# First-layer weight chunks of 256 inputs by 512 columns, and a second row buffer, in the first mixture of a one-core kernel

## The chip, the core and the metric

The kernel runs on one core of a Trainium2 chip. The metric is the device time of one execution in microseconds (us), as a median over several runs. The engines of the core are PE (TensorE; PEld is its weight load), ACT (ScalarE), DVE (VectorE), POOL (GpSimd) and SP (SyncE, which issues most DMAs here). Each works through its own queue in order; they meet at semaphores.

## The reference

Attention with a learned position bias (2 batches, 8 heads, 576 positions, 64 wide) gives 1152 tokens of 512 numbers. They go through a first mixture of 8 experts, one expert for each token, and then through a dense two-layer block, called the second mixture in the code:

```python
logits = x @ w_gate                      # 1152 x 8
expert_idx = np.argmax(logits, axis=1)   # one expert for each token, at most 288 tokens each
h = np.maximum(np.einsum('ecd,edf->ecf', disp, w1), 0.0)   # per expert: 512 -> 1024
y = np.einsum('ecf,efd->ecd', h, w2)                       # per expert: 1024 -> 512
out[i] = gate_w[i] * y[expert_idx[i], pos[i]]
...
h = x @ w_in; g = ((clip) of h, squared); out = g @ w_out  # 512 -> 2048 -> 512
```

## The kernel before

The attention takes the first 260 us of the span. The change touches only the first mixture, which follows it. There the tokens are gathered in the order of their experts into `xTh` and `xTl` (inputs on the partitions, four blocks of 128; h is a value rounded to the matmul format fp32r, l the remainder that the rounding leaves). Every weight matrix is used in the same two parts, so each product is made of three: h by h, h by l and l by h.

The weights come in chunks of 128 x 1024 numbers (512 KB), eight for each expert: chunks 0 to 3 are first-layer weights, 4 to 7 second-layer weights. A chunk `n` is loaded into a slot of `stage` (6 slots, `w_dma`), its rounded part is cast into `ring_h` (`w_hi`, mostly on ACT, L899, sometimes on DVE, L897) and its remainder is computed into `ring_l` (`w_lo`, L904, on DVE or POOL); `w_lo` then issues the load of chunk `n + 6` on SP. `hook(s)` does this for chunk `8e + 4 + s`, that is four chunks ahead of PE: hooks 0 to 3 prepare the expert's own second layer, hooks 4 to 7 the next expert's first layer. In the last expert hooks 3 and 4 also start to decode the weights of the second mixture on DVE (L941 to L951).

The number of tokens of an expert is known only on the chip, so each expert has two arms behind a branch. `wide_arm` takes up to 288 tokens: weights are stationary, tokens move, 96 products of 288 columns for each layer. `small_arm` takes up to 128 tokens: the tokens are stationary (copied by `x_pick` from their place in `xTh`, `xTl` to the fixed tiles `xsh`, `xsl`, L1199 and L1200), the weights move; the result `hs` is transposed back (`tr`, four times two blocks of 128 x 128) and evicted as `hTh` (ACT) and `hTl` (DVE), and the second layer runs in eight blocks `f`. In this data experts 0, 1 and 4 are wide, 2, 3, 5, 6 and 7 small. A small arm's last step is the transposed output in bank `psh2`, which ACT (L1179) and DVE (L1181) read.

`mid` stands inside the second layer: it transposes gathered tokens that the next experts need (`x_block`), fills the rest of `xTh`, `xTl` with zeros once (in expert 3's arm, L957 and L958), and calls `x_pick` for the next expert. PE tells the branch unit ahead of time which arm comes next (`guess`). The first chunk holds all 512 inputs by 256 columns of the first layer, so it ends two of the eight blocks of h.

The order of the instructions in this part is written out by hand (`tc.manual_schedule`): what stands first in the code stands first in its engine's queue.

Of the kernel before, what the change touches and what calls it, by code (L numbers as in the profile page):

```python
# [9 lines left out]
F32 = mybir.dt.float32  # L10
F32R = mybir.dt.float32r
# [32 lines left out]
P = 128  # L44
# [6 lines left out]
def tile_attn_moe_moe2(  # L51
# [868 lines left out]
    def w1_at(e, c):  # L920
        n = 8 * e + c
        return [t[n % NR].rearrange("p (k f) -> p k f", k=4) for t in (ring_h, ring_l)]

# [168 lines left out]
    hs = mp1.tile([P, F], F32, name="hs")  # L1092
    xsh = mp1.tile([P, 4, P], F32R, name="xsh")
    xsl = mp1.tile([P, 4, P], F32R, name="xsl")

    def wide_arm(e, r, wins, hook, mid):
        for wi, (c0, cw) in enumerate(wins):
            for f in range(8):
                if wi == 0 and f % 2 == 1:
                    hook(f // 2)  # L1100
                wh, wl = w1_at(e, f // 2)
                ps = psH[f % 4]
                fs = slice(P * (f % 2), P * (f % 2) + P)
                n = 0
                for kd in range(4):
                    xh = xTh[:, kd, ds(r["pe"] + c0, cw)]
                    xl = xTl[:, kd, ds(r["pe"] + c0, cw)]
                    for l, m in ((wh, xh), (wh, xl), (wl, xh)):
                        nc.tensor.matmul(ps[:, 0:cw], l[:, kd, fs], m, start=n == 0, stop=n == 11)  # L1109
                        n += 1  # L1110
                nc.scalar.activation(out=hTh[:, f, 0:cw], in_=ps[:, 0:cw], func=AF.Relu)
                nc.vector.scalar_tensor_tensor(out=hTl[:, f, 0:cw], in0=ps[:, 0:cw], scalar=0.0,
                                               in1=hTh[:, f, 0:cw].bitcast(F32), op0=ALU.max, op1=ALU.subtract)
            for f in range(8):
# [16 lines left out]
    def small_arm(e, r, hook, mid):  # L1131
        def tr(c):
            pt = psY[c % 2][:, 0:256]
            for i in range(2):
                f = 2 * c + i
                nc.tensor.transpose(pt[:, P * i:P * i + P], hs[:, P * f:P * f + P], ident)
            p2 = pt.rearrange("p (i t) -> p i t", i=2)
            hv = hTh[:, 2 * c:2 * c + 2, 0:P]
            nc.scalar.copy(out=hv, in_=p2)
            nc.vector.tensor_tensor(out=hTl[:, 2 * c:2 * c + 2, 0:P], in0=p2, in1=hv.bitcast(F32), op=ALU.subtract)  # L1140

        for c in range(4):
            wh, wl = w1_at(e, c)
            ps = psH[c][:, 0:256]
            n = 0
            for kd in range(4):
                xh, xl = xsh[:, kd, :], xsl[:, kd, :]
                for l, m in ((xh, wh), (xh, wl), (xl, wh)):
                    nc.tensor.matmul(ps, l, m[:, kd, :], start=n == 0, stop=n == 11)  # L1149
                    n += 1  # L1150
            nc.scalar.activation(out=hs[:, 256 * c:256 * c + 256], in_=ps, func=AF.Relu)
            if c > 0:
                tr(c - 1)
            hook(c)
# [8 lines left out]
        for f in range(6):  # L1163
            for hf in range(2):
                y_mm(f, hf)
            if f == 0:
                tr(3)
            if f in HK:
                hook(HK.index(f) + 4)
            if f == 3:  # L1170
                mid()
        for hf in range(2):
# [10 lines left out]
    with tc.manual_schedule():  # L1183
# [13 lines left out]

        def x_pick(r):
            nc.vector.tensor_copy(xsh, xTh[:, :, ds(r["dve"], P)].bitcast(F32))  # L1199
            nc.vector.tensor_copy(xsl, xTl[:, :, ds(r["dve"], P)].bitcast(F32))  # L1200

        done = nx0
        if CAP > 0:
            x_pick(regs[0])
            guess(0)
        for e in range(E if CAP > 0 else 0):
# [20 lines left out]

            def mid(late=True, e=e, first=first, more=more, nxt=regs[e + 1] if e + 1 < E else None):
                if late:
                    first()  # L1230
                for t in more:
                    x_block(t, xb[t])
                if e + 1 == zx_at:
                    zfill_x()
                if e == 1:
                    zfill_y()
                if nxt is not None:
                    x_pick(nxt)

            if CAP > P:  # L1240
# [133 lines left out]
def _arrays(q, k, v, w1, b1, w2, moe_w_gate, moe_w1, moe_w2, moe2_w_in, moe2_w_out):  # L1374
# [41 lines left out]
    for b in range(2):  # L1416
# [34 lines left out]
```

## Time and profile before

| | |
|---|---|
| median of 3 runs | 651.42 us (646.96 to 659.75) |
| the profiled execution | 656.27 us, span of its profile 654.5 us |
| PE busy | 571.0 us, 87% of the span |
| DVE busy | 507.6 us, 78% |
| ACT busy | 363.6 us, 56% |
| POOL busy | 330.9 us, 51% |
| mean granted clock of PE | 0.934 |
| experts 2 to 7 | 334.4 to 444.3 us of the span |

The profile is one execution, recorded instruction by instruction. A line such as L904 is a line of the kernel above; `rl<-raw,rh` says which tile is written and which are read. What stands in square brackets is the time in which the engine did nothing before the instruction, and the instruction of another engine that ended it; "issue" there means that nothing in the profile ended it. [...]

### The profile page before, as it was taken

To read this page: it belongs to the slowest core of one execution; us is meant where nothing else is said; L and a number is where in the kernel's file an instruction comes from. 1 tells how busy PE (TensorE), PEld (TensorE's weight loads), DVE (VectorE), ACT (ScalarE), POOL (GpSimd) and SP (SyncE) were. 2 spreads that over 40 slices of the span, in tenths; PEclk is the share of its full clock that TensorE was granted. 3 is DMA by queue.
4 is the path that set the end of the run, shared out by engine and by line. 5 is a ranking of instruction groups with operands and counts; after the bars stand their busy time and mean duration, and the time that the engine had idled before them with its cause. 6 is when DMAs were issued, how large, how long until landed. Compare 5 with 4: busy or idle time off the path is not lost.

```text
span 654.5 us, 14186 instructions
## 1 busy us (share of the span) xinstructions
PE 571.0 (87%) x5336; PEld 510.8 (78%) x5336; DVE 507.6 (78%) x942; ACT 363.6 (56%) x765; POOL 330.9 (51%) x266
## 2 busy tenths in 40 slices
PE   3766887988979996699998998888989999999996
PEld 3646666767767884498998897888969989988985
DVE  7999999999999744746568766775996888887431
ACT  4776776878869633143557436645654743642620
POOL 3789898999989820534263343311421420420442
PEclk9767799999989975799999899888999999999999
DMA  8497967999879985645458764773233134100012
GB/s 338 85 209 167 164 118 157 181 156 163 174 146 189 158 150 177 238 132 200 157 175 264 242 199 159 258 244 127 82 129 128 66 110 148 65 1 1 2 60 86
DMA packets 116388, 98.26 MB, mean 150 GB/s; under 512 B 98000, under 2 KB 99024, under 8 KB 114256
## 3 DMA queue, kind: packets, MB, share of 16 engines
q1 hardware_dynamic: 114000, 89.96, 54.1%
q0 software_dynamic: 1440, 4.72, 2.1%
q10 hardware_dynamic: 864, 2.47, 1.1%
q8 instruction: 51, 0.84, 0.5%
q14 instruction: 33, 0.27, 0.2%
HBM read 65.15 MB, written 4.72 MB: 107 GB/s over the span
## 4 chain that ended last, share of the span: by engine, by line
PE 44%; DVE 7%; issue 4%; ACT 3%; POOL 1%; POOLq 0%; DVEq 0%; ACTq 0%
PE psh L1307 13%; PE psy L1332 7%; PE psh L1109 7%; PE psy L1123 6%; PE psh L1149 5%; PE psh L1332 5%; PE psy L1160 1%; DVE rl L904 1%; ACT rh L899 1%; DVE on L1042 1%; DVE rt L943 1%; DVE cl L1312 1%; DVE gl L1321 1%; POOL out_dram L1340 1%; ACT rh L948 1%
## 5 line engine op out<-in xcount | busy, mean ns | idle before, releaser
L1317 POOL TENSOR_TENSOR rl<-rl,cl 128x384 f32<-128x384 f32 x48 | 51.4, 1071 | 133.3 <-ACT cl L1316 54.7
L904 POOL TENSOR_TENSOR rl<-raw,rh 128x1024 fp32r<-128x1024 f32 x23 | 59.1, 2573 | 97.3 <-ACT rh L899 78.9
L269 PE MATMUL ab_ps<-Wt,mask 128*128 128x64 f16 x720 | 61.0, 204 | 34.3 <-ACT bs L283 16.2
L399 POOL TENSOR_TENSOR hl<-s,hl 128x576 f16<-128x576 f32 x55 | 81.0, 1477 | 5.3 <-ACT mn L359 2.7
L288 POOL TENSOR_TENSOR bias<-bias,bs 128x256 f32<-128x256 f32 x78 | 74.0, 957 | 17.4 <-ACT bs L283 17.2
L904 DVE TENSOR_TENSOR rl<-raw,rh 128x1024 fp32r<-128x1024 f32 x41 | 62.8, 1540 | 18.4 <-PE psh L1149 8.6
L269 PEld LDWEIGHTS <-mask 128*128 128x128 f16 x720 | 51.5, 104 | 28.0 <-DVE mask L252 22.4
L252 DVE TENSOR_TENSOR mask<-sD,sT 128x1024 f16<-128x1024 f16 x72 | 73.1, 1029 | 0.0
L1307 PE MATMUL psh<-yTh,rh 128*128 128x384 f32 x192 | 65.8, 342 | 0.7 <-ACT yTh L1179 0.7
L1307 PE MATMUL psh<-yTh,rl 128*128 128x384 f32 x192 | 65.3, 340 | 0.0
L1307 PE MATMUL psh<-yTl,rh 128*128 128x384 f32 x192 | 64.6, 340 | 0.0
L270 PEld LDWEIGHTS <-mask 128*128 128x128 f16 x720 | 52.3, 105 | 13.3 <-issue 13.2
L270 PE MATMUL ab_ps<-Wt,mask 128*128 128x64 f16 x720 | 60.6, 203 | 0.0
L899 ACT CAST rh<-raw 128x1024 fp32r<-128x1024 f32 x54 | 55.8, 1053 | 4.1 <-DMA raw<-in_moe_w_dram 2.3
L1313 ACT ACTIVATE rl<-psh,half 128x384 f32<-128x384 f32 x48 | 28.0, 582 | 43.5 <-DVE cl L1312 43.4
L283 ACT ACTIVATE bs<-ab_ps,isa 128x256 f32<-128x256 f32 x78 | 35.6, 471 | 24.8 <-DVE bias L275 22.1
L1321 DVE TENSOR_TENSOR gl<-rl,gh 128x384 fp32r<-128x384 f32 x48 | 26.7, 557 | 29.1 <-ACT gh L1320 28.6
L366 ACT ACTIVATE s<-s,mn 128x576 f32<-128x576 f32 x56 | 43.6, 779 | 1.7
L352 DVE CUSTOM_DVE_ANT_0 s<-s_ps,bias 128x576 f32<-128x576 f32 x56 | 41.8, 747 | 3.0 <-POOL bias L288 2.2
L409 PE MATMUL mi<-V16h,pt 128*128 128x64 f16 (+1 forms) x320 | 40.8, 204 | 2.5 <-DMA pt<-hl 2.4
L410 PE MATMUL mi<-V16l,pt 128*128 128x64 f16 (+1 forms) x320 | 40.1, 201 | 0.8 <-DVE V16l L194 0.8
L409 PEld LDWEIGHTS <-pt 128*128 128x128 f16 (+1 forms) x320 | 32.0, 108 | 11.2 <-issue 4.0
(262 smaller groups left out, 1976.3 us busy)
## 6 DMA issues: line engine op xcount, KB each, us to landing
raw<-in_moe_w_dram SPq DMA_DIRECT2D x60, 512.0 KB, 4.2
raw<-in_moe_w_in_dram SPq DMA_DIRECT2D x8, 1024.0 KB, 4.8
raw<-in_moe_w_out_dram SPq DMA_DIRECT2D x8, 1024.0 KB, 4.8
qraw<-in_q_dram SPq DMA_DIRECT2D x15, 256.0 KB, 4.2
kst<-kraw SPq DMA_DIRECT2D x12, 288.0 KB, 6.0
vraw<-in_v_dram SPq DMA_DIRECT2D x3, 768.0 KB, 8.3
xd<-xt SPq DMA_DIRECT2D x8, 256.0 KB, 2.0
raw<-in_moe_w_dram ACTq DMA_DIRECT2D x4, 512.0 KB, 4.7
```

The costliest lines, as they stand in the source:

```text
L252: nc.vector.tensor_tensor(out=m, in0=win, in1=thr, op=ALU.is_gt)
L269: nc.tensor.matmul(pv[:, :, j], m[:, j, :], W["h"], start=True, stop=False)
L270: nc.tensor.matmul(pv[:, :, j], m[:, j, :], W["l"], start=False, stop=True)
L288: nc.gpsimd.tensor_tensor(out=bv, in0=bv, in1=bs_t.pop((it, c)), op=ALU.add)
L399: eng.tensor_tensor(out=hl[:, 1, 0:S], in0=s, in1=hl[:, 0, 0:S], op=ALU.subtract)
L409: nc.tensor.matmul(o, pt[:, blk, ic], vh, start=blk == 0, stop=False)
L899: nc.scalar.copy(out=ring_h[n % NR], in_=stage[n % NS])
L904: eng.tensor_tensor(out=ring_l[n % NR], in0=stage[n % NS], in1=ring_h[n % NR].bitcast(F32), op=ALU.subtract)
L1109: nc.tensor.matmul(ps[:, 0:cw], l[:, kd, fs], m, start=n == 0, stop=n == 11)
L1307: nc.tensor.matmul(ps, l[:, kd, fs], mv[:, kd, cs], start=i == 0, stop=i == 11)
L1317: nc.gpsimd.tensor_tensor(out=rl, in0=rl, in1=cl, op=ALU.add)
L1332: nc.tensor.matmul(ps, l[:, tsl], mv[:, f % 2, :], start=f == 0 and i == 0, stop=f == 3 and i == 2)
```

## The change

Three things change in the first mixture.

- The host lays out `moe_w1` in chunks of 256 inputs by 512 columns instead of 512 inputs by 256 columns. A chunk has the same size; chunks 0 and 1 now make the first four blocks of h together, chunks 2 and 3 the last four. The wide arm holds four blocks open in four banks over two chunks and evicts them in the second; hooks are called after as many products as before. The small arm makes 24 products of 512 columns instead of 48 of 256, evicts `hs` in two halves instead of four quarters, and transposes it in two groups of four blocks (`tr(0)` after chunk 2, `tr(1)` after block 0 of the second layer).
- The tiles for an expert's rows exist twice, used in turn. Where no gathered tokens are outstanding (`early`, from expert 3 on), `x_pick` of the next expert stands at the head of the arm instead of in `mid`.
- In the small arm `mid` stands after block 2 of the second layer and ahead of hook 6, instead of after block 3.

```diff
     def w1_at(e, c):
         n = 8 * e + c
-        return [t[n % NR].rearrange("p (k f) -> p k f", k=4) for t in (ring_h, ring_l)]
+        return [t[n % NR].rearrange("p (k f) -> p k f", k=2) for t in (ring_h, ring_l)]
...
-    xsh = mp1.tile([P, 4, P], F32R, name="xsh")
-    xsl = mp1.tile([P, 4, P], F32R, name="xsl")
+    xs = [[mp1.tile([P, 4, P], F32R, name=f"xs{w}{i}") for w in "hl"] for i in range(2)]
 
     def wide_arm(e, r, wins, hook, mid):
         for wi, (c0, cw) in enumerate(wins):
...
+            for c in range(4):
+                wh, wl = w1_at(e, c)
+                for fb in range(4):
+                    if wi == 0 and fb == 2:
+                        hook(c)
+                    f = 4 * (c // 2) + fb
+                    ps = psH[fb]
+                    fs = slice(P * fb, P * fb + P)
+                    n = 0
+                    for k in range(2):
+                        xh = xTh[:, 2 * (c % 2) + k, ds(r["pe"] + c0, cw)]
+                        xl = xTl[:, 2 * (c % 2) + k, ds(r["pe"] + c0, cw)]
+                        for l, m in ((wh, xh), (wh, xl), (wl, xh)):
+                            nc.tensor.matmul(ps[:, 0:cw], l[:, k, fs], m, start=c % 2 == 0 and n == 0, stop=c % 2 == 1 and n == 5)
+                            n += 1
+                    if c % 2 == 1:
+                        nc.scalar.activation(out=hTh[:, f, 0:cw], in_=ps[:, 0:cw], func=AF.Relu)
...
     def small_arm(e, r, hook, mid):
...
+        xsh, xsl = xs[e % 2]
+
+        def tr(g):
+            for i in range(4):
+                f = 4 * g + i
+                nc.tensor.transpose(psY[g][:, P * i:P * i + P], hs[:, P * f:P * f + P], ident)
+            p4 = psY[g].rearrange("p (i t) -> p i t", i=4)
+            hv = hTh[:, 4 * g:4 * g + 4, 0:P]
+            nc.scalar.copy(out=hv, in_=p4)
+            nc.vector.tensor_tensor(out=hTl[:, 4 * g:4 * g + 4, 0:P], in0=p4, in1=hv.bitcast(F32), op=ALU.subtract)
 
         for c in range(4):
             wh, wl = w1_at(e, c)
-            ps = psH[c][:, 0:256]
+            ps = psH[c // 2]
             n = 0
-            for kd in range(4):
-                xh, xl = xsh[:, kd, :], xsl[:, kd, :]
+            for k in range(2):
+                xh, xl = xsh[:, 2 * (c % 2) + k, :], xsl[:, 2 * (c % 2) + k, :]
                 for l, m in ((xh, wh), (xh, wl), (xl, wh)):
-                    nc.tensor.matmul(ps, l, m[:, kd, :], start=n == 0, stop=n == 11)
+                    nc.tensor.matmul(ps, l, m[:, k, :], start=c % 2 == 0 and n == 0, stop=c % 2 == 1 and n == 5)
                     n += 1
-            nc.scalar.activation(out=hs[:, 256 * c:256 * c + 256], in_=ps, func=AF.Relu)
-            if c > 0:
-                tr(c - 1)
+            if c % 2 == 1:
+                nc.scalar.activation(out=hs[:, 512 * (c // 2):512 * (c // 2) + 512], in_=ps, func=AF.Relu)
+            if c == 2:
+                tr(0)
             hook(c)
...
             if f == 0:
-                tr(3)
+                tr(1)
+            if f == 2:
+                mid()
             if f in HK:
                 hook(HK.index(f) + 4)
-            if f == 3:
-                mid()
...
-        def x_pick(r):
-            nc.vector.tensor_copy(xsh, xTh[:, :, ds(r["dve"], P)].bitcast(F32))
-            nc.vector.tensor_copy(xsl, xTl[:, :, ds(r["dve"], P)].bitcast(F32))
+        def x_pick(e):
+            for dst, src in zip(xs[e % 2], (xTh, xTl)):
+                nc.vector.tensor_copy(dst, src[:, :, ds(regs[e]["dve"], P)].bitcast(F32))
...
+            early = done >= NTT and not more and not pre
...
-                if nxt is not None:
-                    x_pick(nxt)
+                if e + 1 < E and not early:
+                    x_pick(e + 1)
...
                     guess(e + 1)
+                    if early and e + 1 < E:
+                        x_pick(e + 1)
                     small_arm(e, r, lambda s: hook(s, few=True), mid)
                 with few.Else():
                     guess(e + 1)
+                    if early and e + 1 < E:
+                        x_pick(e + 1)
                     first()
                     wide_arm(e, r, windows, hook, lambda: mid(False))
...
-        "moe_w1": c(moe_w1.reshape(8, 4, 128, 4, 256).transpose(0, 3, 2, 1, 4).reshape(8, 4, 128, 1024)),
+        "moe_w1": c(moe_w1.reshape(8, 2, 2, 128, 2, 512).transpose(0, 4, 1, 3, 2, 5).reshape(8, 4, 128, 1024)),
```

## Rows read from the trace of the kernel before

**Rows 1.** The page, shares of the chain that ended last, by engine.
```profile
PE 44%; DVE 7%; issue 4%; ACT 3%; POOL 1%; POOLq 0%; DVEq 0%; ACTq 0%
```

**Rows 2.** Windows of small experts: length, busy PE, PEld, DVE, ACT, POOL, clock, DMA.
```profile
334.40:350.50 16.10, 14.10 (x116) 13.66 (x117) 11.57 (x13) 11.53 (x20) 6.80 (x4) 1.00 0.77 252
350.50:365.20 14.70, 13.25 (x108) 12.79 (x108) 12.82 (x15) 10.55 (x18) 5.21 (x2) 1.00 0.82 264
...
395.20:410.10 14.90, 13.22 (x108) 12.78 (x108) 10.36 (x11) 10.56 (x18) 5.21 (x2) 1.00 0.46 161
410.10:426.80 16.70, 14.67 (x108) 14.15 (x109) 13.09 (x15) 10.56 (x18) 5.20 (x2) 0.90 0.78 257
426.80:444.30 17.50, 15.08 (x108) 14.37 (x108) 12.70 (x15) 8.54 (x16) 2.54 (x3) 0.90 0.72 251
```

**Rows 3.** Timeline of PE, 350 to 441 us: start, length, instruction, idle time before it.
```profile
350.51 0.35 PE L1149 MATMUL psh<-rh,xsh 128*128 128x256 f32 x1 [1.66 <-DVE xsh L1199]
...
365.28 0.37 PE L1109 MATMUL psh<-xTh,rh 128*128 x1 [1.22 <-DVE xTh L957]
...
370.13 0.30 PE L1109 MATMUL psh<-xTh,rh 128*128 x1
...
395.27 0.35 PE L1149 MATMUL psh<-rh,xsh 128*128 128x256 f32 x1 [2.66 <-issue]
...
410.13 0.36 PE L1149 MATMUL psh<-rh,xsh 128*128 128x256 f32 x1 [1.34 <-DVE xsh L1199]
...
440.49 0.39 PE L1160 MATMUL psy<-rh,hTl 128*128 128x256 f32 x1 [0.75 <-DVE hTl L1140]
```

**Rows 4.** Source view, PE's prefetch hints at the head of two arms: shortest/median/longest ns, when.
```profile
L1447 PEldq BRANCH_PREFETCH_HINT  x1: 44/44/44, 395.1 to 395.1; - x1
...
L1447 PEldq BRANCH_PREFETCH_HINT  x1: 30/30/30, 408.8 to 408.8; - x1
```

**Rows 5.** Source view of L904 on DVE: shortest/median/longest in ns.
```profile
L904 DVE TENSOR_TENSOR rl<-raw,rh x41: 1207/1225/2987, 271.5 to 437.0; 128x1024 fp32r<-128x1024 f32 x41
```

**Rows 6.** Timelines of DVE and POOL in expert 5, 400 to 412 us.
```profile
401.70 2.00 DVE L904 TENSOR_TENSOR rl<-raw,rh 128x1024 fp32r<-128x1024 f32 x1 [0.52 <-ACT rh L899]
...
404.63 2.80 POOL L904 TENSOR_TENSOR rl<-raw,rh 128x1024 fp32r<-128x1024 f32 x1 [2.01 <-ACT rh L899]
...
405.53 4.12 DVE L904 TENSOR_TENSOR rl<-raw,rh 128x1024 fp32r<-128x1024 f32 x2
409.57 0.41 DVE L1199 CAST xsh<-xTh 128x512 fp32r x1
```

**Rows 7.** Timeline of DVE in expert 4: it reads the output of expert 3.
```profile
369.12 0.68 DVE L1181 TENSOR_TENSOR yTl<-psh,yTh 128x512 f32 x1
```

**Rows 8.** Timeline of DVE in expert 7, 438 to 440 us.
```profile
438.16 0.68 DVE L941 TENSOR_SCALAR rt<-raw 128x1024 uint32<-128x1024 uint32 x1
438.88 1.23 DVE L943 SCALAR_TENSOR_TENSOR rt<-raw,rt 128x1024 uint32<-128x1024 uint32 x1
```

**Rows 9.** The chain that ended last, in order of time: start, length, products of a piece.
```profile
350.51 3.13 PE psh L1149 x24
353.87 1.44 PE psh L1149 x12
...
426.82 4.64 PE psh L1149 x24
...
535.57 10.88 PE psh L1332 x48
```

**Rows 10.** Window of 2 us in expert 6, columns as in the windows above.
```profile
412.00:414.00 2.00, 1.60 (x9) 1.51 (x8) 0.79 (x2) 1.21 (x2) 0.00 (x0) 0.50 0.93 322
```

**Rows 11.** Groups of instructions by line: busy us, mean ns of one, idle before.
```profile
L899 ACT CAST rh<-raw 128x1024 fp32r<-128x1024 f32 x54 | 55.8, 1053 | 4.1 <-DMA raw<-in_moe_w_dram 2.3 <-PE psy L1123 1.7
L881 ACT CAST xTh<-psh 128x512 fp32r<-128x512 f32 x9 | 5.0, 595 | 15.8 <-PE psh L878 11.6 <-DVE rl L904 4.2
```

More of the change, by code (lines that the diff above doesn't have):

```diff
@@ L1092, in tile_attn_moe_moe2 @@
     hs = mp1.tile([P, F], F32, name="hs")
-    xsh = mp1.tile([P, 4, P], F32R, name="xsh")
-    xsl = mp1.tile([P, 4, P], F32R, name="xsl")
+    xs = [[mp1.tile([P, 4, P], F32R, name=f"xs{w}{i}") for w in "hl"] for i in range(2)]
     def wide_arm(e, r, wins, hook, mid):
         for wi, (c0, cw) in enumerate(wins):
[L1098 to L1104, printed above, removed]
-                for kd in range(4):
[L1106 to L1113, printed above, removed]
@@ new lines, in wide_arm @@
+            for c in range(4):
[15 more added lines that the diff above has]
+                        nc.scalar.activation(out=hTh[:, f, 0:cw], in_=ps[:, 0:cw], func=AF.Relu)
+                        nc.vector.scalar_tensor_tensor(out=hTl[:, f, 0:cw], in0=ps[:, 0:cw], scalar=0.0,
+                                                       in1=hTh[:, f, 0:cw].bitcast(F32), op0=ALU.max, op1=ALU.subtract)
@@ L1131, in small_arm @@
     def small_arm(e, r, hook, mid):
[L1132 to L1140, printed above, removed]
+        xsh, xsl = xs[e % 2]
[7 more added lines that the diff above has]
+            nc.vector.tensor_tensor(out=hTl[:, 4 * g:4 * g + 4, 0:P], in0=p4, in1=hv.bitcast(F32), op=ALU.subtract)
         for c in range(4):
             wh, wl = w1_at(e, c)
-            ps = psH[c][:, 0:256]
+            ps = psH[c // 2]
             n = 0
-            for kd in range(4):
-                xh, xl = xsh[:, kd, :], xsl[:, kd, :]
+            for k in range(2):
+                xh, xl = xsh[:, 2 * (c % 2) + k, :], xsl[:, 2 * (c % 2) + k, :]
                 for l, m in ((xh, wh), (xh, wl), (xl, wh)):
-                    nc.tensor.matmul(ps, l, m[:, kd, :], start=n == 0, stop=n == 11)
+                    nc.tensor.matmul(ps, l, m[:, k, :], start=c % 2 == 0 and n == 0, stop=c % 2 == 1 and n == 5)
                     n += 1
-            nc.scalar.activation(out=hs[:, 256 * c:256 * c + 256], in_=ps, func=AF.Relu)
-            if c > 0:
-                tr(c - 1)
+            if c % 2 == 1:
+                nc.scalar.activation(out=hs[:, 512 * (c // 2):512 * (c // 2) + 512], in_=ps, func=AF.Relu)
+            if c == 2:
+                tr(0)
             hook(c)
@@ L1196, in guess @@
                 tc.mark_branch_hint_location(f"arm{e}", hint=many[e], engines=[mybir.EngineType.PE])
-        def x_pick(r):
-            nc.vector.tensor_copy(xsh, xTh[:, :, ds(r["dve"], P)].bitcast(F32))
-            nc.vector.tensor_copy(xsl, xTl[:, :, ds(r["dve"], P)].bitcast(F32))
+        def x_pick(e):
+            for dst, src in zip(xs[e % 2], (xTh, xTl)):
+                nc.vector.tensor_copy(dst, src[:, :, ds(regs[e]["dve"], P)].bitcast(F32))
         done = nx0
         if CAP > 0:
-            x_pick(regs[0])
+            x_pick(0)
             guess(0)
@@ L1226, in first, with mid @@
                     x_block(t, xb[t])
-            def mid(late=True, e=e, first=first, more=more, nxt=regs[e + 1] if e + 1 < E else None):
+            early = done >= NTT and not more and not pre
+            def mid(late=True, e=e, first=first, more=more, early=early):
                 if late:
```

## The prediction, written before the change was run

> **What bounds the kernel now.** I read the page's shares of the chain first: TensorE is the engine that the span is made of [rows 1]. Then the windows, one for each of the five small experts of the first mixture (2, 3, 5, 6, 7) [rows 2]: the reader is to see that such an expert takes 14.7 to 17.5 us, that PE is busy in all but some 1.5 to 2.4 us of each, and that DVE (10 to 13 us) comes next. So a small expert is PE work plus a pause at its start. The timeline of PE [rows 3] gives that pause and its releaser: expert 3 begins after 1.66 us without a product, expert 6 after 1.34 and expert 7 likewise, all released by the copy of the expert's rows into `xsh`; expert 4 after 1.22, released by the zero fill of `xTh`; expert 5 after 2.66, released by nothing shown. That last one is not a wait for data: the hint that PE issues on entering an arm comes at 395.1, just ahead of the first product at 395.27, whereas that of the next arm comes at 408.8, when its first product is still 1.3 us away [rows 4]. So after a small expert PE stands in the next arm and waits for DVE, and after a wide one the branch itself is late. Why DVE is late stands in its timeline [rows 6]: two remainders of weights (L904) start at 405.53 and last 4.12 us together, because POOL does a third from 404.63 to 407.43, and the copy into `xsh` is queued behind them.
>
> **Part 1, wider products.** Each small expert has 48 products of 256 columns; 12 take 1.44 us [rows 9], so 48 take 5.76. They become 24 of 512 columns; the second mixture runs 48 of those in 10.88 us, 0.227 each [rows 9], so 5.44. Gain 0.32 an expert, **-1.6** for five; the number of columns is the same, so no more is to be had. [...] Wide experts (0, 1, 4) keep their 96 first-layer products of 288 columns in another order, and all DMA sizes stay: nothing.
>
> **Part 2, the row copy.** From expert 3 on, the copy for the next expert stands at the head of the arm and into the other buffer, so it no longer follows the weight remainders; in expert 2 it stays in `mid`, but `mid` moves ahead of hook 6, so one remainder (1.23 us alone, [rows 5]) goes behind it. (That remainder's load on SP, of the chunk six further on, also leaves later; its cast comes most of an arm later, which hides it.) Then expert 3 can start 1.1 us earlier (a remainder less in front, a little lost to the transposes that still end the arm); experts 6 and 7 at once, since PE is in the arm already [rows 4]: 1.3 each; expert 4's zero fill also moves ahead of one remainder: 1.2. Together **-4.9**. The chunks needed first are ready: the remainder on POOL ends at 407.43 [rows 6], ahead of 408.8. Expert 5 gains nothing, its branch being late anyway. At the head of an arm the two copies (0.41 us each, [rows 6]) delay DVE's first remainder by 0.8; that is needed only by the second layer, over 5 us later, which hides it.
>
> **Part 3, fewer and larger evictions in a small arm.** Counted from the arm's start: chunks 0 to 2 take 18 x 0.227 = 4.1, four transposes 0.4, chunk 3 1.4, so the second layer starts at 5.9. ACT evicts 512 columns in about 0.6 (a copy of that size, [rows 11]), DVE the remainder of it in 0.68 (the same size, L1181 in [rows 7]). ACT's queue from the end of chunk 1 (2.8): relu to 3.4, hook 1's cast (1.05, [rows 11]) to 4.5, the copy of the first transposed half from 4.6 to 5.2, hook 2's cast to 6.3. The first half is done at about 6.0, a wait of some 0.1. The second half is where the cover gets thin. Its relu follows hook 2's cast and comes about 0.1 too late; its remainder is now needed by block 4 of 8 instead of block 6, and in DVE's queue it stands behind two weight remainders, of which the first is slowed by POOL to 2.00 [rows 6]. From a cast that ends at 6.3: 6.3 + 2.0 + 1.2 + 0.7 = 10.2, against PE's arrival at 9.8. I take 0.4 of waiting in each of experts 2, 3, 5, 6: **+1.6**. The bounds: nothing, if the casts come earlier (hook 0 no longer follows a relu), and 0.4 + 1.8 = 2.2 each, 8.8 in all, where the remainder takes the longest time seen, 2.99 instead of 1.23 [rows 5].
>
> In expert 7 hook 3 adds two decode steps of the second mixture (0.68 and 1.23, [rows 8]) ahead of that remainder, which is why PE stopped 0.75 us there already [rows 3], at block 6. With the remainder needed at block 4, six to twelve products earlier, the stop becomes 0.4 + 1.9 = 2.3 less a little, against 0.75: **+1.3**, bounds 0 and 2.5.
>
> **Part 4, a new wait in expert 4.** It is wide and follows a small one. Before, its third block, the first into bank `psh2`, came after 24 products; now after 12, 1.6 us in. That bank holds expert 3's output until L1181 has read it, which DVE does at 369.12 to 369.80 [rows 7], behind the zero fill, hook 6, and hook 7's cast and remainder, all of which stay in front of it; only the two row copies leave (-0.7). PE, without a product since 364.06 [rows 3], would come to it at 364.1 + 1.6 = 365.7 (12 products of 288 columns, scaled from 0.120 for 256) and go on at 369.1: **+3.4**, so the gain at this start is given back threefold. Before, PE came to it at 370.13 [rows 3] and met no wait. The bounds are 0, if the queue in front shrinks, and 3.4. Behind the waiting block stand the other products of the arm alone; ACT and DVE then have less to do.
>
> **The clock.** In expert 7 the first 24 products took 4.64 us, in expert 3 3.13 [rows 9]: 1.5 lost. [...] In expert 4 the first 24 products took 4.85 (365.28 to 370.13, [rows 3]), much the same. With the pauses of 6 and 7 gone I expect full clock there: **-3.0**; bounds 0 and -3.0. Expert 4 swaps one pause for a longer one, so I expect its slow stretch to stay, 0 (bound -1.5).
>
> **Sum:** -1.6 - 4.9 + 1.6 + 1.3 + 3.4 - 3.0 = -3.2 us. The profiled execution took 656.3, so 653.1; it lies 4.9 above the median of 651.4, and I apply the difference to the median: **648**.
>
> **Rivals.** *The clock stays as it was* (or the branch takes the place of the copy in front of experts 6 and 7, so that the change doesn't do what it says there): two short pauses remain at each boundary, for the output's two copies. The sum loses its 3.0: 651. For it speaks that expert 3 had the longest of the copy's pauses and no slow stretch, so pauses alone do not settle it; against the branch speak the hints [rows 4].
>
> *DVE becomes the bound inside the small arm; slower.* Its place is the remainder of the second half of hT, needed at block 4; its price is each microsecond by which that comes later than in part 3, times four arms, and 3.2/4 = 0.8 more in each wipes out the gain. At the 2.2 of the upper bound the sum is -3.2 + 7.2 = +4.0, 655; with the clock lost too, 658. The trace has remainders on DVE of 2 to 3 us beside POOL [rows 5, 6]. [...] Against it: POOL's and DVE's order in the arm is unchanged, and there the row says 2.00.
>
> *More gain:* expert 4's wait is short, or its slow stretch goes, and the arms wait for nothing: -1.6 - 4.9 + 1.3 - 4.5 with the bank's wait at 0 is -9.7, 642.
>
> **How the numbers follow.** Forecast 0.45, clock or branch stays 0.25, slower 0.15, more gain 0.15. The outer cases give 642 and 658, and the runs before spread from 647 to 660 without any change; to leave out 2 in 10 the range is 640 to 657. 2% (13 us) is about what a measurement of this kernel can tell from no change. No case reaches it by itself; a case at an end together with that spread does: faster 0.06, same 0.88, slower 0.06.
>
> **What would show it.** In the profile of the changed kernel: 12 first-layer products of 512 columns in about 2.7 us; experts 3, 6 and 7 starting within some 0.3 us of the last transpose, not released by `xsh`; PE waiting about 3 us in expert 4 for L1181's successor on DVE, after 12 products; a stop of about 2 us in expert 7 and of a few tenths in the other small arms, released by `hTl`; full clock in experts 6 and 7. I am wrong if the pauses at the starts are still there with another releaser, if expert 4 runs through, or if the small arms stop for over a microsecond. The code of an arm gets shorter, which can move stops of PE that are released by nothing shown, like that before expert 5; I have no row for that and leave it at nothing, within the range.

## The result, and the profile after

The changed kernel took 642.21 us in the median (639.36 to 655.75, 5 runs), the kernel before 650.68 beside it (646.96 to 659.75, 5 runs): ratio 0.9857, 95% interval 0.9808 to 0.9905. Forecast were 648, a range of 640 to 657 and a gain of 3.2; the time lies within the range, and the gain is 8.5, more than twice the forecast. A second series of the changed kernel (`a_again` below) gave 0.9934, 0.9896 to 0.9971. How far apart two series can lie shows the kernel before, run against itself as `b_again`: 1.0073. So the times alone tell apart what differs by more than 0.7%, and I lean on the traces for the rest.

The profiled execution of the changed kernel took 655.75 us and was a disturbed one; its stops can be read, its total can't, and totals of the changed kernel are taken from `a_again` (640.83 us).

The page of the profile after; first the span, then busy time by engine, then the shares of the chain, as in [rows 1]:

```profile
span 654.0 us, 13899 instructions
...
PE 574.3 (88%) x5216; PEld 505.4 (77%) x5216; DVE 503.3 (77%) x932; ACT 361.0 (55%) x745; POOL 329.8 (50%) x266
...
PE 43%; DVE 7%; ACT 4%; issue 4%; POOL 1%; POOLq 0%; DVEq 0%; ACTq 0%
```

The shares of the chain move by a point at most. The timeline of PE does; these are all stops of over 0.7 us in the first mixture after its first product, to be held against [rows 3]:

```profile
333.12 0.47 PE L1152 MATMUL psh<-rh,xsh 128*128 128x512 f32 x1 [1.62 <-DVE yTl L1129]
...
348.99 0.75 PE L1152 MATMUL psh<-rh,xsh 128*128 128x512 f32 x1 [1.51 <-DVE rl L904]
...
368.80 0.41 PE L1110 MATMUL psh<-xTh,rh 128*128 x1 [2.56 <-DVE yTl L1185]
...
396.54 0.54 PE L1152 MATMUL psh<-rh,xsh 128*128 128x512 f32 x1 [1.98 <-ACT rh L899]
...
437.82 0.58 PE L1164 MATMUL psy<-rh,hTl 128*128 128x256 f32 x1 [1.95 <-DVE hTl L1143]
```

In order: starts of experts 2 and 3, the bank in expert 4, the start of expert 5, `hTl` in expert 7. The starts of experts 4, 6 and 7 (364.41, 412.07, 425.94) have no stop any more; before, they had 1.22, 1.34 and 1.32. Expert 3's start still has one, with another releaser, L904. Is it a wait for that remainder? The source view of the hint that PE issues on entering an arm, and the timeline of DVE:

```profile
L1457 PEldq BRANCH_PREFETCH_HINT  x1: 35/35/35, 348.8 to 348.8; - x1
```

```profile
347.06 0.41 DVE L1204 CAST xsh<-xTh 128x512 fp32r x1
347.39 0.41 DVE L1204 CAST xsl<-xTl 128x512 fp32r x1
347.73 1.21 DVE L904 TENSOR_TENSOR rl<-raw,rh 128x1024 fp32r<-128x1024 f32 x1
```

The rows are copied by 347.80 and PE's last transpose ended at 347.48, yet PE enters the arm only at 348.8 and multiplies 0.2 later. The arm is entered late, as before expert 5 in [rows 4]; the releaser named, L904, merely ended near by. In the kernel before, PE entered this arm in time, at 348.8, just as its last product ended (348.85), and waited for the copy alone. So a late arm has come here in place of the copy.

The same stops in `a_again`, another execution of the same kernel:

```profile
322.63 0.47 PE L1152 MATMUL psh<-rh,xsh 128*128 128x512 f32 x1 [1.56 <-ACT rh L899]
...
339.38 0.47 PE L1152 MATMUL psh<-rh,xsh 128*128 128x512 f32 x1 [2.41 <-DVE rh L897]
...
357.57 0.40 PE L1110 MATMUL psh<-xTh,rh 128*128 x1 [2.57 <-DVE yTl L1185]
...
384.62 0.47 PE L1152 MATMUL psh<-rh,xsh 128*128 128x512 f32 x1 [1.33 <-ACT yTh L1127]
...
424.36 0.39 PE L1164 MATMUL psy<-rh,hTl 128*128 128x256 f32 x1 [1.93 <-DVE hTl L1143]
```

Three of the five, the starts, name a different releaser in each execution (L1129 and L899, L904 and L897, L899 and L1127); the bank and `hTl` name the same one both times. Releasers that change are a sign that none of them is the cause.

### The profile page after: what moved, and what is told of

Read it like the earlier page. It is cut to its first block, busy times and chain, and to the rows that moved or that the text cites. A ratio compares the mean times of both kernels' runs of the same rounds, so it can differ in the third digit from the quotient of the medians.

```text
span 654.0 us, 13899 instructions
## 1 busy us (share of the span) xinstructions
PE 574.3 (88%) x5216; PEld 505.4 (77%) x5216; DVE 503.3 (77%) x932; ACT 361.0 (55%) x745; POOL 329.8 (50%) x266
## 4 chain that ended last, share of the span: by engine, by line
PE 43%; DVE 7%; ACT 4%; issue 4%; POOL 1%; POOLq 0%; DVEq 0%; ACTq 0%
PE psh L1317 12%; PE psy L1342 7%; PE psh L1110 6%; PE psy L1125 6%; PE psh L1342 5%; PE psh L1152 4%; ACT rh L899 2%; PE psy L1164 2%; DVE rl L904 1%; DVE on L1042 1%; DVE rt L943 1%; DVE gl L1331 1%; DVE cl L1322 1%; POOL out_dram L1350 1%; ACT rh L948 1%
## 5 line engine op out<-in xcount | busy, mean ns | idle before, releaser
L904 POOL TENSOR_TENSOR rl<-raw,rh 128x1024 fp32r<-128x1024 f32 x23 | 57.8, 2514 | 93.8 <-ACT rh L899 76.5
L269 PE MATMUL ab_ps<-Wt,mask 128*128 128x64 f16 x720 | 62.0, 205 | 31.5 <-ACT bs L283 13.5
L269 PEld LDWEIGHTS <-mask 128*128 128x128 f16 x720 | 52.3, 105 | 26.0 <-DVE mask L252 21.4
L904 DVE TENSOR_TENSOR rl<-raw,rh 128x1024 fp32r<-128x1024 f32 x41 | 62.4, 1535 | 6.5 <-ACT rh L899 5.2
L270 PEld LDWEIGHTS <-mask 128*128 128x128 f16 x720 | 53.2, 106 | 12.5 <-issue 12.4
L270 PE MATMUL ab_ps<-Wt,mask 128*128 128x64 f16 x720 | 61.6, 205 | 0.0
L899 ACT CAST rh<-raw 128x1024 fp32r<-128x1024 f32 x54 | 55.8, 1050 | 5.0 <-DMA raw<-in_moe_w_dram 2.9
```

The lines of the kernel that those rows point to most:

```text
L269: nc.tensor.matmul(pv[:, :, j], m[:, j, :], W["h"], start=True, stop=False)
L270: nc.tensor.matmul(pv[:, :, j], m[:, j, :], W["l"], start=False, stop=True)
L899: nc.scalar.copy(out=ring_h[n % NR], in_=stage[n % NS])
L904: eng.tensor_tensor(out=ring_l[n % NR], in0=stage[n % NS], in1=ring_h[n % NR].bitcast(F32), op=ALU.subtract)
```

## Where the time is: one table for all kernels

For each kernel I took one window of its profile, from the first product of expert 0 to the first of the second mixture: its length, PE's busy time in it, the rest of it (length less busy time), and its mean granted clock (the profile gives it as a share of full speed, 1.00). The attention in front, the same code in all, starts expert 0 anywhere from 264.6 to 276.4 us, so a whole span says less than this window.

| kernel | median us (runs) | ratio to before, interval | mixture | PE busy | rest | clock |
|---|---|---|---|---|---|---|
| before | 650.68 (5) | | 168.8 | 153.4 | 15.4 | 0.95 |
| `b_again`, before once more | 654.17 (11) | 1.0073, 1.0033 to 1.0112 | 169.2 | 153.0 | 16.2 | 0.96 |
| changed | 642.21 (5) | 0.9857, 0.9808 to 0.9905 | 167.3 | 155.4 | 11.9 | 0.95 |
| `a_again`, changed once more | 641.67 (11) | 0.9934, 0.9896 to 0.9971 | 162.4 | 150.3 | 12.1 | 0.98 |
| `c_chunks` | 645.72 (12) | 0.9968, 0.9931 to 1.0005 | 168.1 | 155.0 | 13.1 | 0.95 |
| `d_rows` | 652.76 (12) | 1.0016, 0.9978 to 1.0055 | 169.0 | 152.9 | 16.1 | 0.96 |
| `e_bank` | 638.82 (6) | 0.9836, 0.9787 to 0.9885 | 162.2 | 153.0 | 9.2 | 0.96 |
| `f_split` | 649.88 (12) | 1.0013, 0.9978 to 1.0047 | 171.9 | 154.0 | 17.9 | 0.96 |
| `g_decode` | 644.34 (9) | 0.9941, 0.9898 to 0.9983 | 162.3 | 151.7 | 10.7 | 0.97 |
| `h_bank_decode` | 640.79 (6) | 0.9864, 0.9810 to 0.9918 | 159.8 | 150.9 | 8.9 | 0.97 |
| `j_before_straight` | 637.31 (6) | 0.9844, 0.9809 to 0.9880 | 158.0 | 148.4 | 9.6 | 0.99 |
| `m_rows_straight` | 636.10 (6) | 0.9816, 0.9764 to 0.9869 | 154.9 | 149.0 | 5.9 | 0.98 |
| `i_after_straight` | 637.58 (6) | 0.9833, 0.9793 to 0.9873 | 157.5 | 150.3 | 7.2 | 0.97 |
| `k_split_straight` | 636.47 (6) | 0.9838, 0.9795 to 0.9881 | 157.9 | 149.9 | 8.0 | 0.98 |

## The experiments

### First round: is the gain in the mixture at all, and in which half of the change?

`a_again` is the changed kernel, unedited.

> The changed kernel a second time, for its times and for a second profile. Theory 1, the gain is made in the first mixture (wider products, no copy in front of experts 6 and 7, and no half-clock stretch there): 6 to 9 us below the kernel before again, and the stretch from expert 0 to the second mixture takes 161 to 165 us instead of the 168.8 of before (444.4 - 275.6). Theory 2, the mixture gains some 1.5 us only, as the first two profiles say (167.3 after), and the rest of the 8.5 us is where the half-clock stretches of the attention happened to fall: 0 to 4 us below before, and the stretch takes 166 to 168 us.

Measured: 641.67 us; the mixture is 162.4 us, 6.4 and 6.8 shorter than in the two profiles of the kernel before. The gain is in the mixture.

`c_chunks` keeps the new chunks and products, but one row buffer (`xs[0]` throughout), no early copy, and `mid` where it was:

```diff
-    xs = [... for i in range(2)]
+    xs = [... for i in range(1)]
-            early = done >= NTT and not more and not pre
+            early = False
-            if f == 2:
-                mid()
...
+            if f == 3:
+                mid()
```

> The chunks and wide products alone; the row copy has one buffer and stays in mid, mid stays behind block 3. Theory 1: the pauses in front of experts 3, 6 and 7 released by the row copy are back (1.3 us each or more), the bank wait of expert 4 is shorter or gone because the start is late again, the wait for hTl in expert 7 stays near 2 us; 0 to 3 us below before. Theory 2 (nothing in the mixture matters much, the clock does): the same as the full change within 3 us.

`d_rows` is the other half: the kernel before, with the second row buffer, the early copy and the earlier `mid`, on the old chunks and 256-column products.

> The row copy's second buffer, its early place and the earlier mid alone, on the chunks of before. Theory 1: experts 6 and 7 start at once, no stops inside the small arms, expert 7's wait for hTl 0.8 us as before, and expert 4 meets its third block after 24 products, 3.2 us in, so its bank wait is about 1.5 us instead of 2.6; 3 to 7 us below before. Theory 2: within 3 us of before.

Measured: 645.72 and 652.76 us, ratios 0.9968 (0.9931 to 1.0005) and 1.0016 (0.9978 to 1.0055). Neither half alone can be told from the kernel before by its time. The mixture of `c_chunks` is as long as before (168.1), with less of the rest (13.1 against 15.4 and 16.2) and a busy time of 155.0, against 153.4 and 153.0; that of `d_rows` hardly differs from before. In `c_chunks` the copy into `xsh` (L1204 there) still holds experts 6 and 7, but for half as long as in [rows 3]; PE's timeline:

```profile
338.64 0.47 PE L1152 MATMUL psh<-rh,xsh 128*128 128x512 f32 x1 [1.77 <-ACT rh L899]
...
402.76 0.47 PE L1152 MATMUL psh<-rh,xsh 128*128 128x512 f32 x1 [0.61 <-DVE xsh L1204]
...
417.18 0.47 PE L1152 MATMUL psh<-rh,xsh 128*128 128x512 f32 x1 [0.61 <-DVE xsh L1204]
```

In `d_rows` the copy holds only expert 3, by 0.53 instead of 1.66. But look at expert 6, PE's timeline again:

```profile
348.10 0.36 PE L1150 MATMUL psh<-rh,xsh 128*128 128x256 f32 x1 [0.53 <-DVE xsh L1201]
...
409.04 0.47 PE L1150 MATMUL psh<-rh,xsh 128*128 128x256 f32 x1 [4.04 <-issue]
...
413.54 0.37 PE L1150 MATMUL psh<-rh,xsl 128*128 128x256 f32 x1 [1.89 <-issue]
```

Its first product comes after 4.04 us, and ahead of the last of the same bank's 12 products PE stands for 1.89 more. "issue" says that nothing in the profile released either. Its hint comes at 408.8. Expert 6 there takes 19.3 us to the start of expert 7, against 16.7 and 18.0 before. So it seems that freeing PE from the copy only let it run earlier into a stop that has no data behind it; the third round tests this.

`e_bank` takes away the new wait of part 4: the transposed output goes to the other bank, which the next expert needs only in its second layer.

```diff
-            nc.tensor.transpose(psH[2][:, P * m:P * m + P], ys[:, P * m:P * m + P], ident)
-        p4 = psH[2].rearrange("p (m t) -> p m t", m=4)
+            nc.tensor.transpose(psY[1][:, P * m:P * m + P], ys[:, P * m:P * m + P], ident)
+        p4 = psY[1].rearrange("p (m t) -> p m t", m=4)
```

> The changed kernel with a small arm's output transposed into bank psy1 instead of psh2, so that expert 4's third block doesn't wait for the reader of expert 3's output. If that wait is a price: no stop in expert 4 after 12 products (2.6 us in the profile of the changed kernel), and no half-clock stretch behind it; 2.5 to 4 us below the changed kernel. If the wait only uses up slack (DVE's queue is late anyway): the stop moves to another wait for DVE in expert 4, and the time is that of the changed kernel within 1 us.

Measured: 638.82 us, ratio 0.9836, against `a_again`'s 0.9934 beside it. Windows from the first product of expert 4 to that of expert 5; `e_bank`, then `a_again`:

```profile
355.22:382.84 27.62, 25.99 (x193) 25.64 (x193) 19.04 (x30) 11.77 (x20) 10.62 (x4) 1.00 0.65 226
```

```profile
353.16:384.62 31.46, 27.56 (x194) 27.12 (x193) 18.94 (x29) 11.47 (x20) 10.62 (x4) 0.95 0.58 198
```

3.8 us: the wait of 2.57, and the rest mostly with the clock, which was 0.95 over the window with the wait and 1.00 over the one without. The whole mixtures differ by 0.2 only (162.2 and 162.4): the rest falls by 2.9, and PE's busy time is 2.7 longer, at a mean clock of 0.96 against 0.98.

### Second round: the number of products, and expert 7

`f_split` is the changed kernel with each first-layer product of a small arm cut into two of 256 columns, as before, and two relus of 256; chunks, rows and everything else stay changed.

```diff
-                    nc.tensor.matmul(ps, l, m[:, k, :], start=c % 2 == 0 and n == 0, stop=c % 2 == 1 and n == 5)
+                    for hf in range(2):
+                        nc.tensor.matmul(psH[2 * (c // 2) + hf][:, 0:256], l, m[:, k, 256 * hf:256 * hf + 256],
+                                         start=c % 2 == 0 and n == 0, stop=c % 2 == 1 and n == 5)
```

> The changed kernel with each 512-column product of the small arms made as two of 256 into two banks (and two relus of 256 for one of 512). If the width is worth what the rows of before gave (0.32 us an expert), 1.6 us above the changed kernel and no new stops. If the gain of the chunks lies in the shorter code of an arm (24 products and weight loads fewer), stops of PE released by nothing shown come back at the branches and inside experts 6 and 7, as in the kernel with the row copy alone (4.0 and 1.9 us there): 4 to 8 us above the changed kernel.

Measured: 649.88 us, ratio 1.0013. The whole gain is gone, for a term that I had put at 1.6: 8.2 us by the medians of two series on two chips (649.88 - 641.67), some 5 by their ratios. PE's timeline says where; three stops that neither profile of the changed kernel has:

```profile
298.47 0.40 PE L1110 MATMUL psh<-xTl,rh 128*128 x1 [1.38 <-issue]
...
329.73 0.39 PE L1152 MATMUL psh<-rl,xsh 128*128 128x256 f32 x1 [1.23 <-issue]
...
408.16 0.53 PE L1152 MATMUL psh<-rh,xsh 128*128 128x256 f32 x2 [3.09 <-issue]
```

All three are inside an arm, among its first-layer products, and released by nothing. The first is in expert 1, which is wide and whose code is the changed kernel's. So it doesn't look like the width as such, but like what the longer code of a small arm does to stops of PE. (The halves also take the bank `psh2`, which the changed kernel's small arms leave to the output; expert 3 waits 0.83 us for it, and that is the edit's own price.)

`g_decode` moves the four decode steps of the second mixture one hook later, so that none stands ahead of expert 7's second remainder; `h_bank_decode` is this and `e_bank` together.

```diff
-                if NCH - 1 <= n < NCH + 1:
-                    for k in (0, 1) if n < NCH else (2, 3):
+                if NCH <= n < NCH + 2:
+                    for k in (0, 1) if n == NCH else (2, 3):
```

> The changed kernel with the first two decode steps of the second mixture at hook 4 of the last expert instead of hook 3, the next two at hook 5. If PE's wait for hTl in expert 7 (1.95 us) is what these steps cost, it falls to some 0.3 us, expert 7 gets 1.5 to 2 us shorter, and so does the time. If the steps are needed as early for the second mixture, the wait moves to its first products or to the decode chain behind them, and the time stays within 0.7 us.

> Both: output in psy1 and the decode steps one hook later. If both waits are prices of their own, the gains add: 4 to 6 us below the changed kernel, 10 to 13 below the kernel before, and expert 4 takes about 27.6 us, expert 7 about 16 or less. If one only uncovers the other's slack, no better than the bank alone.

Measured: 644.34 and 640.79 us. In `g_decode` the stop for `hTl` (1.93) is gone, but another is there, at the end of expert 7; PE's timeline:

```profile
426.26 0.71 PE L1181 MATMUL psh<-cst,hs 128*128 128x128 f32 x4 [1.59 <-ACT hs L1179]
```

ACT's copy of the output stands behind the cast of the decoded weights (L948), which ends about as late in the expert as in `a_again` (14.2 and 14.1 us after its first product); there PE comes later, held by `hTl`, and meets 0.22 of this wait. Expert 7 takes 15.90 us against 16.35 in `a_again`: 0.45 won of 1.93. The times don't tell `g_decode` from the changed kernel, nor `h_bank_decode` from `e_bank`; the latter two are the fastest versions with both arms. Both beat the kernel before; the changed kernel's series of the same kind (0.9934) `e_bank` beats by 1.0%, `h_bank_decode` by 0.7%, the edge of what the times tell.

`b_again` is the kernel before, unedited.

> The kernel before against itself, for a second profile of it and for what the comparison makes of no change: a ratio whose interval holds 1.000, half as wide as 0.004 to 0.006; the stretch from expert 0 to the second mixture 166 to 169 us (168.8 in its first profile), with the pause in front of experts 3, 6 and 7 and a stop of 1 to 2 us early in expert 1.

Measured: 654.17 us, ratio 1.0073 where 1 was expected. Its profile, a second one of the same kernel, is worth more than its time. PE's timeline:

```profile
305.30 0.29 PE L1109 MATMUL psh<-xTh,rh 128*128 x1 [1.70 <-issue]
...
367.14 0.37 PE L1109 MATMUL psh<-xTh,rh 128*128 x1 [1.10 <-DVE yTl L1181]
...
392.48 0.35 PE L1149 MATMUL psh<-rh,xsh 128*128 128x256 f32 x1 [2.70 <-issue]
```

The stops without a releaser are there again, in the middle of expert 1 and ahead of expert 5. And the wait for the bank, which I called new, is in the kernel before too: 1.10 us after 24 products. In the profile that I predicted from, PE ran most of those products at half clock (4.85 us for the 24, at a mean clock of 0.65; here they took 3.56) and came too late to meet it.

### Third round: the same kernels without branches

If late arms are the cause, they must vanish with the branches. The data of this case always takes the same arms, so I left out the others, and with them the branches and the hints; the order of all other instructions stays. (Such a kernel computes the mixture only for routings like this one.)

```diff
-                with tc.If(cnts[e] < P + 1, preferred_fallthrough_block=False, label=f"arm{e}") as few:
-                    guess(e + 1)
...
+            if e not in (0, 1, 4):
                     small_arm(e, r, lambda s: hook(s, few=True), mid)
-                with few.Else():
-                    guess(e + 1)
...
+            else:
                     wide_arm(e, r, windows, hook, lambda: mid(False))
```

> Leaves out the same arms, branches and hints from the kernel before. Theory 1: the stops that nothing releases, 1.6 us in expert 1 and 2.7 ahead of expert 5, vanish; those for xsh and xTh ahead of experts 3, 4, 6 and 7 (1.2 to 1.7 each) stay, as a wait for DVE doesn't depend on code; the time falls by about 4 to 5 us, ratio 0.993. Theory 2: ratio 1.00, and the stop ahead of expert 5 stays.

> Leaves out the arms that this data doesn't take (experts 0, 1, 4 only wide, the others only small), with the branches and hints; the order of the rest is the changed kernel's. Theory 1 (PE starts experts 2, 3 and 5 late because the branch and the code behind it arrive late): these three stops, 1.3 to 2.4 us each in the changed kernel, fall below 0.3, the bank's wait in expert 4 (2.6) and the hTl stop of expert 7 (1.9) stay, and the time is 4 to 6 us under the changed kernel, ratio to the kernel before about 0.978. Theory 2 (those stops are waits for the casts and evictions that the profile names as releasers, L899, L897, L1129): they stay at 1.3 us or more, ratio about 0.987.

> The changed kernel with each wide product of a small arm as two of 256 columns, and without the untaken arms, branches and hints. With branches this split cost 8 us. Theory 1 (the products' number costs by the code that PE must get behind a branch): without branches only the width itself is left, 0.3 us an expert, so the time lies within 2 us of the straight changed kernel, ratio about 0.981. Rival (the products' number costs by itself, by issue or by the second relu): it stays 6 to 8 us above the straight changed kernel, ratio about 0.99.

> The second row buffer, early copy and earlier mid alone, on the kernel before's chunks, without the untaken arms, branches and hints. With branches it gained nothing. Theory 1 (the copy's pauses do go, but late code takes their place behind a branch): without branches the gain predicted for this part shows, 4.9 less the bank's wait of about 1.5, so 3 to 4 us under the straight kernel before, ratio about 0.988, with experts 3, 4, 6 and 7 starting within 0.5 us. Rival (the copy was never what held these starts): the same time as the straight kernel before.

Measured: 637.31, 637.58, 636.47 and 636.10 us, beside 647.37 for the kernel before on the same chip. All four intervals overlap almost wholly. Without branches the kernel before is as fast as the changed one, within what the times tell, and the split, which cost 5 to 8 us, costs nothing. Theory 1 holds, though the kernel before gains 10.1 us where I expected 4 to 5; the rival of `k_split_straight` (issue, or the second relu) falls with it. The gain that I expected of `m_rows_straight` over `j_before_straight` is too small for the times, but the windows have it (154.9 against 158.0).

The stops that remain, PE's timelines. The kernel before, straight:

```profile
338.56 0.39 PE L1149 MATMUL psh<-rh,xsh 128*128 128x256 f32 x1 [1.44 <-DVE xsh L1199]
...
353.29 0.40 PE L1109 MATMUL psh<-xTh,rh 128*128 x1 [1.09 <-DVE xTh L957]
...
357.96 0.40 PE L1109 MATMUL psh<-xTh,rh 128*128 x1 [1.01 <-DVE yTl L1181]
...
395.07 0.39 PE L1149 MATMUL psh<-rh,xsh 128*128 128x256 f32 x1 [1.13 <-DVE xsh L1199]
...
409.92 0.38 PE L1149 MATMUL psh<-rh,xsh 128*128 128x256 f32 x1 [1.20 <-DVE xsh L1199]
...
422.14 0.39 PE L1160 MATMUL psy<-rh,hTl 128*128 128x256 f32 x1 [0.69 <-DVE hTl L1140]
...
424.62 0.71 PE L1177 MATMUL psh<-cst,hs 128*128 128x128 f32 x4 [1.04 <-ACT hs L1175]
```

The changed kernel, straight:

```profile
353.93 0.39 PE L1164 MATMUL psy<-rh,hTl 128*128 128x256 f32 x1 [0.82 <-DVE hTl L1143]
...
362.00 0.40 PE L1110 MATMUL psh<-xTh,rh 128*128 x1 [2.70 <-DVE yTl L1185]
...
424.79 0.38 PE L1164 MATMUL psy<-rh,hTl 128*128 128x256 f32 x1 [1.88 <-DVE hTl L1143]
```

The rows alone, straight:

```profile
342.11 0.39 PE L1150 MATMUL psh<-rh,xsh 128*128 128x256 f32 x1 [0.30 <-DVE xsh L1201]
...
346.04 0.38 PE L1150 MATMUL psh<-rh,xsh 128*128 128x256 f32 x1 [0.48 <-DVE yTl L1182]
...
361.35 0.40 PE L1108 MATMUL psh<-xTh,rh 128*128 x1 [1.47 <-DVE yTl L1182]
```

No stop is left without a releaser, none at experts 2 and 5, and every one that is left has the releaser that the code gives it. Here, with nothing late in front, the terms of the prediction can be read off cleanly. Expert 0 to 7 in the two straight kernels take 158.0 and 157.5 us; the windows of the kernel before and of its straight form:

```profile
272.20:441.40 169.20, 153.04 (x1141) 148.99 (x1141) 111.69 (x149) 85.71 (x148) 59.46 (x29) 0.96 0.63 205
```

```profile
268.00:426.00 158.00, 148.40 (x1140) 145.03 (x1140) 112.47 (x149) 85.52 (x148) 60.20 (x29) 0.99 0.65 218
```

So the branches cost the kernel before 11.2 us of its mixture (169.2 - 158.0), `f_split` 14.0 (171.9 - 157.9, its straight form), and the changed kernel 4.9 (162.4 - 157.5). The change gains 6.8 us of mixture with the branches and 0.5 without them. The medians say the same, 10.1 us for the kernel before (647.37 - 637.31) and 4.1 for the changed one (641.67 - 637.58, from two series; by the ratios 1.6 to 6.6).

These windows are single executions, and not all of the difference is arms that are late. The column "rest", in which PE does nothing, is the safer measure: leaving out the branches takes 6.6 us off it in the kernel before, 9.9 in `f_split`, 10.2 in `d_rows` and 4.9 in the changed kernel, and the change gains 4.1 of it with branches and 2.4 without. The other 4.6 of the 11.2 us are PE's busy time, at a clock of 0.96 with the branches and 0.99 without; between the two profiles of the changed kernel alone busy time differs by 5.1 us (155.4 at 0.95 and 150.3 at 0.98). Slow stretches after expert 0 are rarer without branches (one in four profiles, at least one in each of the ten others), but how much of the clock the late arms cost isn't shown.

What an arm waits for is not in the profile by name. But the page has a queue of instruction transfers (count, MB, share); the kernel before, then straight:

```profile
q8 instruction: 51, 0.84, 0.5%
```

```profile
q8 instruction: 42, 0.69, 0.4%
```

The changed kernel has 49, `f_split` 51 again; in the mixture alone they are 18, 16 and 18, and 9 or 10 in the straight kernels. That is some 16 KB each (0.84 MB over 51). The trace also keeps when each transfer started and how long it took (0.9 to 1.8 us), and the stops can be held against that:

| kernel, stop of PE | idle us | last transfer of the queue | PE goes on | after the transfer's end |
|---|---|---|---|---|
| before, in expert 1, no releaser | 1.57 | 305.54 to 306.45 | 308.01 | 1.56 |
| before, start of expert 5, no releaser | 2.66 | 392.56 to 393.53 | 395.27 | 1.74 |
| `a_again`, start of expert 2 | 1.56 | 320.01 to 320.94 | 322.63 | 1.69 |
| `a_again`, start of expert 3 | 2.41 | 336.75 to 337.67 | 339.38 | 1.71 |
| `d_rows`, start of expert 6, no releaser | 4.04 | 406.36 to 407.75 | 409.04 | 1.29 |
| `d_rows`, in expert 6, no releaser | 1.89 | 411.32 to 412.28 | 413.54 | 1.26 |
| `f_split`, in expert 6, no releaser | 3.09 | 405.75 to 406.71 | 408.16 | 1.45 |
| before, start of expert 3, `xsh` | 1.66 | 338.67 to 339.80 | 350.51 | 10.71 |
| `a_again`, the bank in expert 4 | 2.57 | 341.39 to 342.35 | 357.57 | 15.22 |

It is so throughout. The ten profiles with branches have 37 stops of 0.35 us or more inside the mixture that name no releaser or stand at the start of expert 2, 3 or 5 with one that isn't `xsh`; every one of them ends 1.26 to 1.83 us after such a transfer. Of the 50 other stops of that length in the 14 profiles, the waits for data, none does. So I take late arms, and the stops inside them, for waits for code, by these times alone.

Which arm is late depends on more than the length of the code: expert 3 is late in every profile of the new chunks with 84 products and transposes in a small arm (by 1.31 to 2.41 us), and in none of the kernel before, and `f_split` and the kernel before, with 108 each, stop at different places. Length and place against these transfers were not told apart; an edit that moves the code and keeps its length was not run. What the traces show is transfers of some 16 KB, stops that end 1.26 to 1.83 us behind one, at entering an arm and in the middle of one, and no such stop where nothing is skipped; how the code is fetched they don't show. The straight kernels drop the branches and the skipped code at once, so which of the two counts is not told apart.

## Why the prediction was right in the number, and where its working failed

**The step that failed is the last one: "The code of an arm gets shorter ... leave it at nothing".** A small arm's products and transposes go from 108 to 84 ([rows 2] for the first count; a window of `a_again` has 84 or 85), and most of the gain goes with the late code: the change gains 6.8 us of mixture with the branches and 0.5 without them (in PE's stops alone 4.1 and 2.4; the other part is clock). Putting the products back (`f_split`) loses the whole gain with branches and nothing without. I had the sign of it in [rows 3] and [rows 4], 2.66 us ahead of expert 5 with no releaser and a hint just before the first product, and took it as given ("its branch being late anyway"). "Wide experts ... nothing" falls by the same: expert 1, from its first product to expert 2's, takes 28.0 us in `a_again`, 29.8 and 29.7 before, as its stop without a releaser (1.6 to 1.7) is gone.

**Width, -1.6.** By itself right: 18 products of 512 columns took 4.11 us in the straight changed kernel, 36 of 256 columns 2.88 + 1.44 = 4.32 in the straight kernel before, so 0.28 an expert and -1.4. "No more is to be had" was wrong with branches, as `f_split` shows. The chains of these two, the changed one first:

```profile
328.97 4.11 PE psh L1152 x18
```

```profile
322.95 2.88 PE psh L1149 x24
...
326.05 1.44 PE psh L1149 x12
```

**Row copy, -4.9.** As a stop it is right: 1.44 + 1.09 + 1.13 + 1.20 = 4.9 in the straight kernel before, 0.30 with the rows alone. As a gain it is half right: with branches experts 4, 6 and 7 start at once, but expert 3 is entered late (1.51 and 2.41 us). The rival "the branch takes the place of the copy" put this in front of experts 6 and 7; on the old chunks (`d_rows`) it is so for expert 6, on the new ones for neither.

**Small arms, +1.6.** Too much: no stop over 0.3 inside experts 2, 3, 5 and 6 in `a_again`; 0.82 in expert 3 alone in the straight kernel. In expert 5 there the remainder was done 9.8 us into the arm, as PE came to it, where I had put 10.2. The rival of a slower kernel (DVE as the bound) needed 0.8 more in each of four arms; it falls.

**Expert 7, +1.3.** Right: 1.93 in `a_again` against 0.75 in [rows 3], so +1.2, at the remainder named. What I overlooked gives most of it back: at the end of expert 7 the kernel before waits 1.04 us for ACT's copy of the output (442.98, L1177; the straight one likewise, above), the changed one 0.22.

**Bank in expert 4, +3.4.** The place and the releaser are right, the size is not: 2.57, of which the kernel before has 1.0 to 1.1 where its first 24 products take 3.6 to 3.7 us (`b_again`, and straight) instead of 4.85, so +1.5. That PE "met no wait" was true of one execution.

**Clock, -3.0.** Right in place: over the first 24 products of expert 7 the kernel before has a mean clock of 0.63, over those of expert 3 1.00, and [rows 10] has 0.50 in expert 6; `a_again` shows 1.00 over experts 6 and 7. The price is a matter of the execution, though: `i_after_straight` has a slow stretch in expert 7 (clock 0.90 from 412.9 to 430.5), `b_again` one in expert 6 alone (0.81 from 407.3 to 425.3). Every slow stretch that I found in these mixtures after expert 0 lies at or just behind a stop of PE (1.2 to 4.0 us); not every stop has one.

Without the clock the prediction's terms make -0.2. As measured, without the code, they give -1.4 - 4.9 + 0.8 + 1.2 + 1.7 = -2.6 (the bank by the straight pair, 2.70 - 1.01); the two straight windows differ by 0.5, and expert 7's slow stretch lies in the one that would have been ahead. So for the work that it priced the sum of -3.2 was near, but by errors that cancel, and the measured gain is mostly of something else: that the time fell within the range is luck in part. The rival with more gain gave the very time, 642, but by another way: its arms that wait for nothing are there, its short wait in expert 4 isn't.

## What to carry to other kernels

Where work stands behind branches, count the instructions of an arm as a cost of their own: fewer, larger instructions can pay several times what their own timeline promises (here the split cost 5 to 8 us with branches, where the width by itself is worth 1.4), and a copy or wait that is taken away may only uncover a late arm (4.04 us ahead of expert 6 in `d_rows`). Read the releaser of a stop at an arm's start in two executions and look at when the engine enters the arm; a releaser that changes, or that ends after the data needed, is hardly the cause. Then look at when the last instruction transfer ended. And before a wait is called new, look for it in a second profile of the kernel before.

## What the runs showed of the hardware

PE stood for 0.4 to 4.0 us for nothing that the profile names as releaser, not only when it entered an arm but inside an arm's first-layer products (1.23, 1.38, 1.89, 3.09 us), in a mixture with eight two-armed branches; without them no such stop was left in the mixture in four kernels. These stops, and the late starts of arms with a releaser that changes, ended 1.26 to 1.83 us after a 16 KB transfer of the instruction queue, 37 of 37, and of 50 waits for data none did. They fall in places that an edit didn't touch, as in expert 1 in `f_split` (1.38 us). Leaving out the arms not taken, with their branches, made the kernel before 1.6% faster (ratio 0.9844, 0.9809 to 0.9880), about as much as the change did in the first of its two series (0.9857, then 0.9934).
